# Attention's output normalised instead of its probabilities, with the reciprocals taken through DRAM

## The chip, the cores and the metric

The kernel runs on one core of a Trainium2 chip. The core has five engines with queues of their own that work in order: TensorE (PE: matmuls and transposes, into PSUM), VectorE (DVE), ScalarE (ACT), GpSimd (POOL) and SyncE (SP), which here only issues DMAs. The metric is device time in microseconds. The kernel before takes 586.34 us, the median of three runs (584.38 to 586.84).

## The reference

Causal attention over 2 batches x 12 heads, 448 tokens, head size 64; its output, as 896 rows of 768, goes through two dense blocks.

```
scores = q @ k.T / 8;  masked above the diagonal
attn   = exp(scores - max);  attn = attn / (sum(attn) + 1e-9)
x      = attn @ v                        # 896 x 768
h      = ((x @ w1) * (x @ w2)) @ w3 @ w_out
h      = h @ w_in;  out = (h * clip(h + 3, 0, 6) / 6) @ w_out2
```

## The kernel before

**Stages.** Attention comes first and ends at about 153 us of the span. Beside it the program multiplies w3 and w_out into one matrix (tile `pw`, written to DRAM as `product_of`), which depends on no activation; these 384 matmuls fill TensorE where attention leaves it free, and go on after it. Then come the products of x with w1 and w2 in a scheme of seven products per block (`pa`, tiles paX, paY, paZ), the product with the combined matrix (`px`), and the two matrices of the last block (`pg`, `po`). The dense stages hold every operand as a high and a low part and run three matmuls per product.

**Attention.** Two heads make a unit; there are twelve units u, six of each batch. A unit has seven tiles t of 64 queries. Its 128 partitions are 64 queries of two heads. `scores` (L392) runs for t = 6 down to 0: a matmul of q's tile with the keys up to it into a PSUM bank `s` (L399); VectorE adds the mask, writes the scores `z` to SBUF and leaves the row's extreme in `sums` (L402); ScalarE takes the exponential into the buffer `prb` and leaves the row's sum in `sums` (L406). `normalise` (L411) is called three times per unit, for tiles 6 and 5, for 4 and 3, and for 2 to 0: VectorE adds 1e-9 and takes the reciprocals (L417, L418), and GpSimd multiplies each tile of `prb` by its column of reciprocals (L425). `p_t` (L435) transposes the 16 blocks of 128x128 on TensorE in four groups (L447) and copies them to `pt` (L455 on ScalarE, L459 on VectorE). `p_v` (L463) multiplies `pt` with v into one PSUM bank `o` (L472), which holds 64 rows of either head and the 448 queries as columns, and turns it into `xt`: a high part on ScalarE (L489) and a low part on VectorE (L490), or plain copies (L487, L494) for the second batch, where the differences of L564 are formed from x itself.

**Weights.** Each weight tile comes as 64-bit numbers (`w3r`, `wrr`, `w1r`, `w2r`) and is converted by ScalarE (L266), VectorE (L269, L271, L273) and split into parts (L250 on ScalarE, L253 on VectorE or GpSimd).

**The order of the work.** Operations are declared with an engine, a cost, what they read and write, and a rank. A planner (`Plan.issue`) plays them through with these costs and hands each engine, whenever it is free, the ready operation of lowest rank. The result is a fixed order for every engine; on the chip each engine follows it and waits where an operand is not there. SP's queue is fixed in the same way: a DMA whose condition isn't met holds up all that stand behind it.

Of the kernel before, what the change touches and what calls it, by code (L numbers as in the profile page):

```python
# [23 lines left out]

GROUPS = (5, 3)
# [127 lines left out]
def attention_moe_moe2(ctx: ExitStack, tc, q, k, v, w1, w2, w3, w_out, v_in, v_out, out):  # L153
# [43 lines left out]
    three, small = consts[:, :1], consts[:, 1:4]  # L197
# [144 lines left out]
    qr, kr, vr, qs, ks, sums, pt, pr = {}, {}, {}, {}, {}, {}, {}, {}  # L342
# [68 lines left out]
    def normalise(u, t0, t1):  # L411
        sm, pb = sums[u], pr[u]
        rank = u + (TQ - t0) * 0.05
        acc = [sm.at((1, t)) for t in range(t0, t1)]

        def go():
            nc.vector.tensor_tensor(sm[:, 2, t0:t1], sm[:, 1, t0:t1], small[:, :t1 - t0], ALU.add)  # L417
            nc.vector.reciprocal(sm[:, 1, t0:t1], sm[:, 2, t0:t1])  # L418

        plan.op("dve", 0.47, go, writes=acc, rank=rank)  # L420

        def scale(t):
            n = (t + 1) * T
            s = pb[:, OFF[t]:OFF[t] + n]
            nc.gpsimd.tensor_tensor(s, s, sm[:, 1, t:t + 1].to_broadcast([P, n]), ALU.mult)  # L425

        for t in reversed(range(t0, t1)):
            plan.op("pool", pool((t + 1) * T), lambda t=t: scale(t),
                    reads=[sm.at((1, t))], writes=[pb.at(t)], rank=rank)
# [32 lines left out]
    def p_v(u):  # L462
# [23 lines left out]
        if b and p < HK:  # L486
            plan.op("act", act(S), lambda: nc.scalar.copy(f32(t[:, 0]), ps[:, :S]), reads=[ps], writes=[t.at(0)], rank=rank)  # L487
        else:
            plan.op("act", act(S), lambda: nc.scalar.copy(t[:, HI], ps[:, :S]), reads=[ps], writes=[t.at(0)], rank=rank)  # L489
            plan.op("dve", dve(S), lambda: nc.vector.tensor_tensor(t[:, LO], ps[:, :S], f32(t[:, HI]), ALU.subtract),  # L490
                    reads=[ps, t.at(0)], writes=[t.at(1)], rank=rank)
        if b and p >= HK:
            bf[p] = plan.tile(lambda: wrp.tile([P, S], F32, tag=f"bf{p}", name=f"bf{p}"), f"bf{p}", 1)
            plan.op("act", act(S), lambda: nc.scalar.copy(bf[p][:, :], ps[:, :S]), reads=[ps], writes=[bf[p]], rank=rank)  # L494
# [3 lines left out]
    for u in range(n_u):  # L498
        load(u)
        top = TQ  # L500
        for t in reversed(range(TQ)):
            scores(u, t)
            if t in (*GROUPS, 0):
                normalise(u, t, top)
                top = t
# [357 lines left out]
```

## Time and profile before

| | us |
|---|---|
| median of three runs | 586.34 (584.38 to 586.84) |
| profiled execution: its own time | 585.28 |
| its span in the trace | 583.5 |
| TensorE busy | 559.1 (96%) |
| VectorE busy | 408.9 (70%) |
| ScalarE busy | 282.4 (48%) |
| GpSimd busy | 147.1 (25%) |

The profiled execution is 1.06 us under the median and 1.8 us over its span. Busy time counts an engine's instructions, including time in which an instruction stands on an engine and waits; TensorE's ends are modelled. A group of instructions is given as line, engine, operation, names and shapes, count, busy time and mean of one, and after the second bar the idle time of the engine ahead of it with what ended it.

### The profile page before, as it was taken

The numbers are of one execution on the slowest core, as the hardware profiler recorded it, in microseconds if no ns is written. First come the engines' busy times: TensorE is split into PE (matmuls) and PEld (weight loads), VectorE is DVE, ScalarE is ACT, GpSimd is POOL, SyncE is SP. The second block draws the span as 40 slices with busy tenths as digits, with TensorE's granted clock in tenths as the row PEclk, the third lists the DMA queues.
The fourth block names the chain that finished last, engine by engine and source line by source line (L and its number), as shares of the span: only waits on it lengthen the run. The fifth ranks groups of instructions, "written<-read, shape, count | busy, mean of one in ns | idle before, by whom it ended". The sixth has DMA issues, their size and how long they took to land.

```text
span 583.5 us, 7873 instructions
## 1 busy us (share of the span) xinstructions
PE 559.1 (96%) x2900; PEld 496.1 (85%) x2900; DVE 408.9 (70%) x691; ACT 282.4 (48%) x532; POOL 147.1 (25%) x143
## 2 busy tenths in 40 slices
PE   7797989899999999999999999999999999999997
PEld 5575666677899998888999999999999999999996
DVE  4989898898795989999845447877878865452000
ACT  5777778777652454554523325555556623130100
POOL 3878787698121223321210000000000000000000
PEclk9889989999999999999999999999999999999999
DMA  8565566543432223432233114333344442440000
GB/s 314 186 207 185 183 243 207 172 169 124 120 123 64 99 109 108 148 115 82 77 123 109 51 58 162 110 108 109 110 144 145 144 158 91 136 144 16 17 31 33
DMA packets 22855, 73.39 MB, mean 126 GB/s; under 512 B 2080, under 2 KB 11296, under 8 KB 20256
## 3 DMA queue, kind: packets, MB, share of 16 engines
q1 hardware_dynamic: 22816, 72.88, 36.4%
q8 instruction: 23, 0.38, 0.3%
q14 instruction: 16, 0.13, 0.1%
HBM read 66.98 MB, written 5.90 MB: 125 GB/s over the span
## 4 chain that ended last, share of the span: by engine, by line
PE 73%; DVE 14%; POOL 3%; DMA 3%; issue 3%; ACT 2%; SPq 0%; DVEq 0%; POOLq 0%; ACTq 0%
PE po L793 20%; PE pg L617 20%; PE px L752 10%; PE pw L535 8%; PE paX L678 4%; PE s L399 4%; POOL prb L425 3%; PE ptp L447 3%; PE o L472 2%; PE paZ L678 2%; DVE z L402 2%; DVE wd L253 2%; DMA ks<-in_k 1%; PE paY L678 1%; DMA w1r<-in_moe_w 1%
## 5 line engine op out<-in xcount | busy, mean ns | idle before, releaser
L793 PE MATMUL po<-g,vo 128*128 128x448 f32 x576 | 115.4, 362 | 0.0
L617 PE MATMUL pg<-x2t,vi 128*128 128x448 f32 x576 | 115.4, 362 | 0.0
L617 PEld LDWEIGHTS pg<-x2t,vi 128*128 128x128 f32 x576 | 108.0, 187 | 7.2
L793 PEld LDWEIGHTS po<-g,vo 128*128 128x128 f32 x576 | 108.0, 187 | 7.2
L425 POOL TENSOR_TENSOR prb<-prb,sums 128x448 f32<-128x448 f32 (+6 forms) x84 | 75.3, 922 | 29.1 <-DVE sums L418 24.9
L535 PE MATMUL pw<-wr,w 128*128 128x384 f32 x384 | 76.6, 349 | 0.0
L535 PEld LDWEIGHTS pw<-wr,w 128*128 128x128 f32 x384 | 66.5, 190 | 1.7 <-issue 0.5
L399 PE MATMUL s<-ks,qs 128*128 128x448 f32 (+6 forms) x168 | 52.5, 425 | 9.7 <-DVE sums L402 7.2
L752 PE MATMUL px<-ab,wp 128*128 128x448 f32 x288 | 57.8, 362 | 0.0
L752 PEld LDWEIGHTS px<-ab,wp 128*128 128x128 f32 x288 | 54.0, 187 | 3.6
L406 ACT ACTIVATE prb<-z,sums 128x448 f32<-128x448 f32 (+6 forms) x84 | 42.2, 506 | 7.2 <-DVE sums L402 7.1
L399 PEld LDWEIGHTS s<-ks,qs 128*128 128x128 f32 x168 | 29.5, 202 | 19.0 <-DVE sums L402 10.0
L402 DVE CUSTOM_DVE_ANT_0 z<-s,maskb 128x448 f32<-128x448 f32 (+6 forms) x84 | 33.1, 418 | 13.6 <-PE s L399 8.6
L638 ACT ACTIVATE r<-pg,consts 128x448 f32<-128x448 f32 x32 | 20.4, 636 | 33.3 <-PE pg L617 33.3
L447 PEld LDWEIGHTS ptp<-ident,prb 128*128 128x128 f32 x192 | 23.0, 146 | 13.9 <-POOL prb L425 9.1
L447 PE MATMUL ptp<-ident,prb 128*128 128x128 f32 x192 | 27.8, 287 | 5.9 <-POOL prb L425 5.8
L455 ACT COPY pt<-ptp 128x512 f32<-128x512 f32 (+1 forms) x48 | 25.1, 562 | 16.4 <-PE ptp L447 16.0
L266 ACT ACTIVATE vor<-vor 128x1024 f32<-128x1024 f32 x12 | 13.9, 1155 | 39.4 <-DMA vor<-in_moe_w_out 39.4
L312 POOL TENSOR_TENSOR w2r<-w2r 128x384 f32<-128x384 f32 x8 | 9.9, 1244 | 74.3 <-DVE w2r L273 51.2
L640 DVE SCALAR_TENSOR_TENSOR g<-r,pg 128x448 f32<-128x448 f32 x32 | 19.8, 619 | 12.5 <-ACT r L638 12.4
L653 DVE COPY out<-po 128x448 f32<-128x448 f32 x6 | 3.7, 624 | 35.3 <-PE po L793 35.1
L472 PE MATMUL o<-pt,vr 128*64 128x448 f32 (+3 forms) x192 | 26.4, 394 | 0.2
(110 smaller groups left out, 890.5 us busy)
## 6 DMA issues: line engine op xcount, KB each, us to landing
vir<-in_moe_w_in SPq DMA_DIRECT2D x16, 768.0 KB, 4.2
vor<-in_moe_w_out SPq DMA_DIRECT2D x12, 1024.0 KB, 5.0
w3r<-in_moe_w SPq DMA_DIRECT2D x8, 1024.0 KB, 5.2
wrr<-in_moe_w_out SPq DMA_DIRECT2D x8, 768.0 KB, 4.5
w1r<-in_moe_w SPq DMA_DIRECT2D x8, 768.0 KB, 5.7
w2r<-in_moe_w SPq DMA_DIRECT2D x8, 768.0 KB, 4.4
qs<-in_q SPq DMA_DIRECT2D x12, 448.0 KB, 3.9
vr<-in_v SPq DMA_DIRECT2D x12, 256.0 KB, 2.7
```

The costliest lines, as they stand in the source:

```text
L399: plan.op("pe", pe4(n), lambda: nc.tensor.matmul(ps[:, :n], qs[u][:, t].rearrange("p h i -> p (h i)"), ks[u][:, :n], start=True, stop=True ...
L402: plan.op("dve", dve(n) + 0.09, lambda: nc.vector.tensor_tensor_reduce(out=z[:, :n], in0=ps[:, :n], in1=maskb[:, S - n:], scale=-SCALE, sc ...
L406: plan.op("act", act(n, True) + 0.2, lambda: nc.scalar.activation(pb[:, OFF[t]:OFF[t] + n], z[:, :n], AF.Exp, bias=sm[:, 0, t:t + 1], scal ...
L425: nc.gpsimd.tensor_tensor(s, s, sm[:, 1, t:t + 1].to_broadcast([P, n]), ALU.mult)
L447: nc.tensor.transpose(ps[:w, i * P:(i + 1) * P], pb[:, OFF[t] + kb * P:OFF[t] + kb * P + w], ident)
L455: plan.op("act", act(cut), lambda: nc.scalar.copy(dst()[:, :cut], ps[:, :cut]), reads=[ps], writes=[d.at((g, 0))], rank=rank)
L472: nc.tensor.matmul(ps[T * j:T * j + T, kb * P:S], vr[u][:w, kb, j, :], d[:w, base[kb]:base[kb] + TQ - 2 * kb, j, :], start=kb == 0, stop=k ...
L535: nc.tensor.matmul(ps[:, :W], weight(n, a, kk), hls[1 + kk][:, c, h * W:(h + 1) * W], start=kk == 0 and a == c, stop=kk == KF - 1 and a == LO)
L617: nc.tensor.matmul(ps[:, :S], weight(n, a, kk), x(kk, c), start=st, stop=sp)
L678: nc.tensor.matmul(ps[:, :S], hl[:, a, off + kk * P:off + (kk + 1) * P], t[:, c], start=first and kk == 0 and a == c, stop=kk == HK - 1 an ...
L752: nc.tensor.matmul(ps[m, b][:, :S], weight(n, a, kk), ab[kk][:, c, cols(b)], start=kk == 0 and a == c, stop=kk == KF - 1 and a == LO)
L793: nc.tensor.matmul(ps[:, :S], weight(n, a, kk), gt[k][:, c, cols(b)], start=k == 0 and a == c, stop=k == KF2 - 1 and a == LO)
```

## The change

The call of `normalise` goes, and with it GpSimd's multiplication of the probabilities: the transposes take the exponentials as they are. Once per unit, behind its seven tiles, `invert` adds 1e-9 to the seven sums and takes their reciprocals on VectorE. They lie with queries along the partitions and are wanted along the columns of `o`; so one DMA writes the 128x7 reciprocals to a piece of DRAM (`line`, 28 bytes from each partition), and two DMAs read it back, one per head, each spreading a row of 448 numbers over 64 partitions (`inv`, in the scratch tag "a2"). In `p_v` VectorE multiplies the bank `o` by `inv`, reading `inv` at a step of seven numbers, and writes x. Where high and low parts are wanted, ScalarE casts x and GpSimd subtracts; for the second batch's first three units x itself is all that is needed.

```diff
--- before.py
+++ after.py
@@ -21,8 +21,6 @@
 
 BANKS = {'s': 3, 'pt': 2, 'o': 1}
 DENSE_BANKS = 2
-
-GROUPS = (5, 3)
 
 AHEAD = 0.5
 
@@ -194,7 +192,7 @@
     dp = ctx.enter_context(tc.tile_pool(name="dp", bufs=1, space=bass.MemoryType.DRAM))
     pd = ctx.enter_context(tc.tile_pool(name="pd", bufs=DENSE_BANKS, space=PSUM))
     consts = cp.tile([P, 8], F32, name="consts")
-    three, small = consts[:, :1], consts[:, 1:4]
+    three, small = consts[:, :1], consts[:, 1:]
 
     ctx.enter_context(tc.manual_schedule())
 
@@ -339,7 +337,7 @@
 
     seq = [(b, p) for b in range(B) for p in range(NP)]
     n_u = len(seq)
-    qr, kr, vr, qs, ks, sums, pt, pr = {}, {}, {}, {}, {}, {}, {}, {}
+    vr, qs, ks, sums, pt, pr, inv = {}, {}, {}, {}, {}, {}, {}
 
     def scratch(tag, name):
         return plan.tile(lambda: xp.tile([P, S], F32, tag=tag, name=name, bufs=2), tag, 2)
@@ -408,25 +406,26 @@
             bias=sm[:, 0, t:t + 1], scale=-1.0, accum_out=sm[:, 1, t:t + 1]),
             reads=[z, sm.at((0, t))], writes=[pb.at(t), sm.at((1, t))], rank=rank + RANK["exp"])
 
-    def normalise(u, t0, t1):
-        sm, pb = sums[u], pr[u]
-        rank = u + (TQ - t0) * 0.05
-        acc = [sm.at((1, t)) for t in range(t0, t1)]
+    def invert(u):
+
+        sm = sums[u]
+        rank = u + (TQ - 1) * 0.05
 
         def go():
-            nc.vector.tensor_tensor(sm[:, 2, t0:t1], sm[:, 1, t0:t1], small[:, :t1 - t0], ALU.add)
-            nc.vector.reciprocal(sm[:, 1, t0:t1], sm[:, 2, t0:t1])
-
-        plan.op("dve", 0.47, go, writes=acc, rank=rank)
-
-        def scale(t):
-            n = (t + 1) * T
-            s = pb[:, OFF[t]:OFF[t] + n]
-            nc.gpsimd.tensor_tensor(s, s, sm[:, 1, t:t + 1].to_broadcast([P, n]), ALU.mult)
-
-        for t in reversed(range(t0, t1)):
-            plan.op("pool", pool((t + 1) * T), lambda t=t: scale(t),
-                    reads=[sm.at((1, t))], writes=[pb.at(t)], rank=rank)
+            nc.vector.tensor_tensor(sm[:, 2], sm[:, 1], small, ALU.add)
+            nc.vector.reciprocal(sm[:, 1], sm[:, 2])
+
+        plan.op("dve", 0.47, go, writes=[sm], rank=rank)
+        line = dp.tile([2, T * TQ], F32, name=f"line{u}")
+        lh = Handle(plan, None, None, 0)
+        lh.ap = line
+        plan.op("sp", 0.6, lambda: nc.sync.dma_start(
+            line.rearrange("j (i t) -> (j i) t", t=TQ), sm[:, 1]), reads=[sm], writes=[lh], rank=rank)
+        inv[u] = scratch("a2", f"inv{u}")
+        for j in range(2):
+            plan.op("sp", 0.6, lambda j=j: nc.sync.dma_start(
+                inv[u][T * j:T * j + T], line[j:j + 1].to_broadcast([T, S])),
+                reads=[lh], writes=[inv[u].at(j)], rank=rank)
 
 
     order = [(kb, t) for kb in range(4) for t in range(2 * kb, TQ)]
@@ -484,25 +483,29 @@
                     writes=[ps], rank=rank)
         t = plan.tile(lambda: xp.tile([P, 2, S], F32R, tag=f"x{p}_{b}", name=f"xt{p}_{b}"), f"x{p}_{b}", 1)
         if b and p < HK:
-            plan.op("act", act(S), lambda: nc.scalar.copy(f32(t[:, 0]), ps[:, :S]), reads=[ps], writes=[t.at(0)], rank=rank)
+            x, write = lambda: f32(t[:, 0]), t.at(0)
+        elif b:
+            bf[p] = plan.tile(lambda: wrp.tile([P, S], F32, tag=f"bf{p}", name=f"bf{p}"), f"bf{p}", 1)
+            x, write = lambda: bf[p][:, :], bf[p]
         else:
-            plan.op("act", act(S), lambda: nc.scalar.copy(t[:, HI], ps[:, :S]), reads=[ps], writes=[t.at(0)], rank=rank)
-            plan.op("dve", dve(S), lambda: nc.vector.tensor_tensor(t[:, LO], ps[:, :S], f32(t[:, HI]), ALU.subtract),
-                    reads=[ps, t.at(0)], writes=[t.at(1)], rank=rank)
-        if b and p >= HK:
-            bf[p] = plan.tile(lambda: wrp.tile([P, S], F32, tag=f"bf{p}", name=f"bf{p}"), f"bf{p}", 1)
-            plan.op("act", act(S), lambda: nc.scalar.copy(bf[p][:, :], ps[:, :S]), reads=[ps], writes=[bf[p]], rank=rank)
+            xf = scratch("a1", f"xf{u}")
+            x, write = lambda: xf[:, :], xf
+        plan.op("dve", dve(S), lambda: nc.vector.tensor_tensor(
+            x().rearrange("p (t i) -> p t i", i=T), ps[:, :S].rearrange("p (t i) -> p t i", i=T),
+            inv[u][:, :].rearrange("p (i t) -> p t i", t=TQ), ALU.mult),
+                reads=[ps, inv[u]], writes=[write], rank=rank)
+        if not b or p >= HK:
+            plan.op("act", act(S, True), lambda: nc.scalar.copy(t[:, HI], x()), reads=[write], writes=[t.at(0)], rank=rank)
+            plan.op("pool", pool(S), lambda: nc.gpsimd.tensor_tensor(t[:, LO], x(), f32(t[:, HI]), ALU.subtract),
+                    reads=[write, t.at(0)], writes=[t.at(1)], rank=rank)
         xt[p, b] = t
 
     setup()
     for u in range(n_u):
         load(u)
-        top = TQ
         for t in reversed(range(TQ)):
             scores(u, t)
-            if t in (*GROUPS, 0):
-                normalise(u, t, top)
-                top = t
+        invert(u)
         for g in range(4):
             p_t(u, g)
         p_v(u)
```

How the orders differ, at three places. `o` and `s` are PSUM banks, `z` the masked scores, `sums` a unit's extremes and sums, `wrr` tiles of weights, `pt` the transposed probabilities. Line numbers after the change are two lower up to L408 and one lower in `p_t` and `p_v` up to L474.

VectorE, around the reciprocals in the middle of attention, before (the additions of one unit stand in three places; the low part of x is taken from `o`):

```order
L402 ISA z_0_526,sums_412<-s_0_471,maskb 128x64
L402 ISA sums_412 128x1
L417 TENSOR_TENSOR sums_412<-sums_412,consts 128x2
L418 RECIPROCAL sums_412<-sums_412 128x2
L402 ISA z_6_540,sums_541<-s_6_477,maskb 128x448
L402 ISA sums_541 128x1
L402 ISA z_5_549,sums_541<-s_5_499,maskb 128x384
L402 ISA sums_541 128x1
L490 TENSOR_TENSOR xt_0_546<-o_506,xt_0_546 128x448
L402 ISA z_4_559,sums_541<-s_4_530,maskb 128x320
```

and after, at the same place:

```order
L400 ISA z_4_552,sums_531<-s_4_527,maskb 128x320
L400 ISA sums_531 128x1
L415 TENSOR_TENSOR sums_419<-sums_419,consts 128x7
L416 RECIPROCAL sums_419<-sums_419 128x7
L493 TENSOR_TENSOR xf_567<-o_482,inv_488 128x448
L267 TENSOR_SCALAR wrr_512<-wrr_512 128x768
L269 SCALAR_TENSOR_TENSOR wrr_416<-wrr_416 128x768
L458 COPY pt_547<-ptp_3_570 64x128
L271 SCALAR_TENSOR_TENSOR wrr_416<-wrr_416 128x768
L400 ISA z_3_605,sums_531<-s_3_549,maskb 128x256
L400 ISA sums_531 128x1
```

The multiplication of one unit's output (`xf` from `o_482` and `inv_488`) stands right behind the reciprocals of the next unit (`sums_419`); behind it come conversions of weights, the copy of pt and the next maximum (z_3).

SP, the queue of one unit in the middle of attention, before:

```order
L244 DMA wrr_444<-in_moe_w_out 128x1536
L359 DMA qs_479<-in_q 128x896
L360 DMA ks_488<-in_k 128x448
L361 DMA vr_524<-in_v 128x512
L244 DMA wrr_537<-in_moe_w_out 128x1536
L244 DMA wrr_579<-in_moe_w_out 128x1536
```

and after:

```order
L422 DMA line_133<-sums_310 128x7
L357 DMA qs_472<-in_q 128x896
L358 DMA ks_479<-in_k 128x448
L426 DMA inv_488<-line_133 64x448
L359 DMA vr_500<-in_v 128x512
L426 DMA inv_488<-line_133 64x448
L242 DMA wrr_512<-in_moe_w_out 128x1536
```

The row to DRAM (`line_133`) stands ahead of the loads of q, k and v of the unit three later (`qs_472`, `ks_479`, `vr_500`), the first spread between k and v, the second behind v.

TensorE, the last output matmuls of attention, before:

```order
L447 MATMUL ptp_3_1603<-ident,prb_88 128x128 x3
L447 MATMUL ptp_3_1603<-ident,prb_88 64x128
L472 MATMUL o_1610<-pt_1584,vr_1243 64x448 x2
L472 MATMUL o_1610<-pt_1584,vr_1243 64x320 x2
L535 MATMUL pw_1_1551<-wr_850,w_1200 128x384 x3
L535 MATMUL pw_1_1551<-wr_861,w_1200 128x384 x3
L535 MATMUL pw_0_1625<-wr_329,w_1309 128x384 x3
L472 MATMUL o_1610<-pt_1584,vr_1243 64x192 x2
L472 MATMUL o_1610<-pt_1584,vr_1243 64x64 x2
```

and after:

```order
L446 MATMUL ptp_2_1473<-ident,prb_88 128x128 x4
L446 MATMUL ptp_3_1482<-ident,prb_88 128x128 x3
L446 MATMUL ptp_3_1482<-ident,prb_88 64x128
L538 MATMUL pw_0_1468<-wr_377,w_1149 128x384 x3
L538 MATMUL pw_0_1468<-wr_490,w_1149 128x384 x3
L471 MATMUL o_1501<-pt_1465,vr_1180 64x448 x2
L471 MATMUL o_1501<-pt_1465,vr_1180 64x320 x2
L471 MATMUL o_1501<-pt_1465,vr_1180 64x192 x2
L471 MATMUL o_1501<-pt_1465,vr_1180 64x64 x2
L538 MATMUL pw_0_1468<-wr_533,w_1149 128x384 x3
```

In the whole order 65 triples of product matmuls (`pw`) stand ahead of attention's last matmul before the change, and 51 after it.

## Rows read from the trace of the kernel before

**Rows 1.** The page, part 1: busy us (share), instructions.

```profile
PE 559.1 (96%) x2900; PEld 496.1 (85%) x2900; DVE 408.9 (70%) x691; ACT 282.4 (48%) x532; POOL 147.1 (25%) x143
```

**Rows 2.** Table by stage: length, busy us, granted clock, DMA share, GB/s.

```profile
5.40:45.00 39.60, 33.92 (x166) 22.58 (x164) 32.97 (x94) 28.55 (x73) 27.57 (x27) 0.87 0.66 238
45.00:100.00 55.00, 48.37 (x278) 34.31 (x276) 49.20 (x137) 42.74 (x114) 43.94 (x44) 0.97 0.61 213
100.00:153.00 53.00, 49.51 (x310) 38.58 (x308) 45.29 (x95) 37.65 (x85) 37.12 (x30) 1.00 0.40 132
153.00:186.00 33.00, 33.00 (x194) 33.00 (x191) 27.37 (x37) 15.00 (x28) 8.42 (x5) 1.00 0.39 120
```

**Rows 3.** The chain that ended last, attention's end: start, us, what.

```profile
152.33 0.74 PE o L472 x8
153.07 32.96 PE pw L535 x189
```

**Rows 4.** TensorE's waits to 150 us: us, times, longest; last line, after.

```profile
PE s L399 <- DVE sums L402: 7.2, 7, 2.2
PE ptp L447 <- POOL prb L425: 5.8, 8, 1.5
...
PE paX L678 <- DVE wa L253: 3.7, 4, 1.4
```

**Rows 5.** Groups on GpSimd to 153 us; last line, from 153 to 300.

```profile
L425 POOL TENSOR_TENSOR prb<-prb,sums 128x448 f32<-128x448 f32 (+6 forms) x84 | 75.3, 922 | 29.1 <-DVE sums L418 24.9 <-DVE sums L417 3.0 <-ACT w3r L266 0.4
L253 POOL TENSOR_TENSOR w<-w3r,w 128x1024 fp32r<-128x1024 f32 x7 | 18.3, 2615 | 2.9 <-ACT w L250 2.9
L253 POOL TENSOR_TENSOR wr<-wrr,wr 128x768 fp32r<-128x768 f32 x8 | 15.5, 1941 | 1.7 <-ACT wr L250 1.7
...
L698 POOL TENSOR_TENSOR u<-u,c 128x448 f32<-128x448 f32 x8 | 11.2, 1399 | 31.3 <-DVE u L696 23.5 <-ACT ab L704 7.8
```

**Rows 6.** VectorE to 153 us, groups; last two, durations ns min/median/max.

```profile
L402 DVE CUSTOM_DVE_ANT_0 z<-s,maskb 128x448 f32<-128x448 f32 (+6 forms) x84 | 33.1, 418 | 13.6 <-PE s L399 8.6 <-ACT prb L406 3.2 <-POOL prb L425 1.2
L417 DVE TENSOR_TENSOR sums<-sums,consts 128x2 f32<-128x2 f32 (+1 forms) x36 | 14.5, 403 | 0.0
L273 DVE SCALAR_TENSOR_TENSOR wrr<-wrr 128x768 uint32<-128x768 uint32 x8 | 11.1, 1390 | 0.0
...
L418 DVE RECIPROCAL sums<-sums 128x2 f32<-128x2 f32 (+1 forms) x36 | 6.1, 170 | 1.2
L490 DVE TENSOR_TENSOR xt<-o,xt 128x448 fp32r<-128x448 f32 x8 | 4.9, 618 | 2.3 <-ACT xt L489 2.3
L459 DVE COPY pt<-ptp 64x128 f32<-64x128 f32 x12 | 3.3, 277 | 2.6 <-ACT pt L455 2.6
...
L273 DVE SCALAR_TENSOR_TENSOR w1r<-w1r 128x768 uint32<-128x768 uint32 x2 | 1.9, 953 | 0.0
...
L417 DVE TENSOR_TENSOR sums<-sums,consts x36: 144/256/1539, 10.5 to 141.7; 128x2 f32<-128x2 f32 x24, 128x3 f32<-128x3 f32 x12
L269 DVE TENSOR_SCALAR w3r<-w3r x8: 678/1047/2148, 9.4 to 131.4; 128x1024 uint32<-128x1024 uint32 x8
```

**Rows 7.** Casts on ScalarE: from PSUM to 153 us; from SBUF, ns min/median/max.

```profile
L489 ACT CAST xt<-o 128x448 fp32r<-128x448 f32 x8 | 4.2, 527 | 6.7 <-PE o L472 6.7
...
L704 ACT CAST ab<-p x8: 565/570/571, 202.8 to 292.3; 128x448 fp32r<-128x448 f32 x8
```

**Rows 8.** SP's wait; k's issue (ns); landings of k, v, product.

```profile
SPq L361 <- PE o L472: 40.4, 9, 6.2
...
L360 SPq DMA_DIRECT2D ks<-in_k x12: 416/424/647, 1.2 to 109.7; - x12
...
DMA to landing us min/median/max: 3.2/4.2/8.1
...
DMA to landing us min/median/max: 2.5/2.7/8.3
...
DMA to landing us min/median/max: 2.0/3.2/5.6
```

## The prediction

> **What bounds the kernel now.** I read the page first: TensorE is busy for 96% of the span [rows 1]. A share of 96% says that no more than 583.5 - 559.1 = 24.4 us of the span is idle time of TensorE, so the next question was where it lies. The table by stage answers [rows 2]: of the 39.6 us from 5.4 to 45 TensorE lacks 5.7, from 45 to 100 it lacks 6.6, from 100 to 153 it lacks 3.5; from 153 to 186 nothing; 3.7 us follow in the next stage, where VectorE's split of wa is late [rows 4]. So 15.8 us lie in the attention stage, which the change is about, and which ends at 153.07 us, where the chain turns into one run of 189 matmuls of the weights' product [rows 3]. [...]
>
> Who made TensorE wait came third [rows 4]: 7.2 us for VectorE's running maxima (the banks of the scores), 5.8 us for GpSimd's scaling of the probabilities (8 waits of the transposes). GpSimd's rows say why it is late: 84 multiplications of 922 ns are 75.3 of its work in the stage [rows 5]. VectorE is the busiest engine of the stage beside TensorE: 33.0 + 49.2 + 45.3 = 127.5 of 147.6 us [rows 2].
>
> **The change part by part.** *TensorE's own work* is the same in kind and number. In the order 195 of the 384 product matmuls stood ahead of attention's last matmul, and 153 do now; the other 42 go behind it, at 32.96/189 = 0.174 us each [rows 3] 7.3 us. That is no gain and no loss: the attention stage ends 7.3 us earlier for it and the run behind it is 7.3 us longer. What counts is idle time and clock.
>
> *GpSimd loses* the 84 multiplications, 75.3 us, and gains nine subtractions of 128x448 (the low parts of x), at 1.4 us of the nearest row, the product of u and c [rows 5], 12.6 us. With the weights' 18.3 + 15.5 its work in the stage falls from about 109 to about 46 us. The 5.8 us that the transposes waited for it [rows 4] go; late next are the exponentials themselves on ScalarE, which stood before GpSimd in the same chain, so that the wait can only shorten. I take -5.8; the bounds are 0 (ScalarE takes its place whole) and -5.8.
>
> *VectorE loses* 24 of 36 pairs of addition and reciprocal. An addition took 403 ns in the mean, though it handles two or three numbers in a lane; its shortest took 144 ns [rows 6], so the rest is standing still until ScalarE's sum is there. 14.5 + 6.1 = 20.6 us become 12 x (0.4 + 0.18) = 7.0: 13.6 us less. Beside GpSimd its other work is slow too: the shift of a w3 tile took 678 ns at the least, 1047 in the median and 2148 at most, with GpSimd's work changing beside it and nothing else in it [rows 6]. Eight such shifts at the median are 8 x 0.37 = 3.0 us over their shortest, and the last joins of wrr 8 x (1.390 - 0.953 of the w1r tiles of the same size) = 3.5 [rows 6]. Of shifts and joins there are six such groups of eight in the stage, so that I take 17 us of excess in all (estimate from these two, with the differences left out); with GpSimd's work at 46/109, 58% of it goes, 10 us. It gains twelve multiplications of the output in place of nine subtractions of 618 ns [rows 6]: 3 x 0.62 = 1.9 us. So VectorE goes from 127.5 to about 106 us of work. Its share of a stage of some 130 us is then 80%, below TensorE's, and I let half of the 7.2 us of waits for the maxima go: -3.6, bounds 0 and -7.2.
>
> The new multiplication reads the reciprocals at a step of 28 bytes; no row shows such a step. Its nearest row is the subtraction from the same bank, 618 ns, and I take that; twice as long would be the upper end, 12 x 0.62 = 7.4 us more on an engine that has some 25 us free, nothing or at most 6.8 us on the path (11 of them in the loop below). [...] Were the multiplication doubled, the sum below would be up to 6.8 us higher; by the row it stays.
>
> *ScalarE* loses the six plain copies of the output (0.53 us each, as its casts [rows 7]) and casts nine times from SBUF instead of from PSUM, 0.57 for 0.53 [rows 7]: -2.8 us, beside other work, nothing on the path.
>
> *The clock.* Lost now: 0.13 x 33.9 + 0.03 x 48.4 = 5.9 us [rows 2]. With fewer idle gaps a part comes back. The loads of the first units stay as late as they are, so I take a third, -2.0; bounds 0 and -5.9.
>
> *The DMAs* are what is added: per unit one of 128 rows of 28 bytes to DRAM and two that spread 1,792 bytes over 64 partitions, 36 in all, at 0.42 us of SP each (k's load [rows 8]), 15 us of SP beside other work. Bytes: 12 x 2 x 64 x 1,792 = 2.75 MB in a stage that moves 132 to 238 GB/s [rows 2], hidden. What can cost is the chain and the queues. On SP the row waits for the reciprocals and the first spread for the row, and loads of q, k and v for the unit three later stand behind and between them. The second spread stands behind that load of v, which waits for the end of this unit's output matmuls: SP already stood 40.4 us behind v in this way [rows 8]. On VectorE the multiplication stands right behind the reciprocal of the next unit, and behind it the conversions, the next maxima and the copy of pt, for which the next output matmul waits. So there is a loop from one unit's output to the next one's: issues of v and of the spread 2 x 0.42, landing 2.7 (v's median [rows 8]), multiplication 0.62, two conversion steps 2.4 (1.39 each beside GpSimd, 0.95 without [rows 6]; I take 1.2), a maximum 0.42, the copy of pt 0.28 [rows 6], the second half of the output matmuls 0.74 [rows 3]: 8.0 us. A unit takes (153.1 - 5.4)/12 = 12.3 us now; on my sum it will take 11.0. So the loop is hidden with 3.0 us to spare, and shows where the spread lands later than 5.7 us. Landings of like DMAs: 2.0 to 5.6 us for the product's stores, 2.5 to 8.3 for v [rows 8]. At 2.0 the cost is nothing; at 8.3 in all eleven turns it is 11 x 2.6 = 29 us. Both rows' medians are near 3, so I take the low end with one or two late landings, +3.0.
>
> *The sum.* 585.28 us is the profiled execution's own time (span 583.5 and 1.8 around it); -5.8 - 3.6 - 2.0 + 3.0 = -8.4 gives 576.9. The median of the three runs is 586.34, 1.06 higher, inside their 584.38 to 586.84; on its scale the forecast is 578.0. Behind 153 us I expect nothing but the shift: the 3.7 us of waits for wa [rows 4] are untouched by the change, and VectorE has 5.6 us free from 153 to 186 [rows 2], with 7.3 us more of the product's run to get ready in.
>
> **The rivals** (all times on the scale of the median).
> 1. The gaps close altogether: -5.8 - 7.2 - 5.9 = -18.9 and no new wait, 567.4. For it: GpSimd loses over half its work, and VectorE with it. Against: in-order engines rarely lose all waits, and the load of k at the start stays.
> 2. The round trip decides: slower. Place: VectorE's multiplication, with the maxima and the copy of pt behind it. If the spreads land after 7.2 us in the mean, 11 x 1.5 = 16.5 us stand in place of the 3.0: 591.5. It wipes out the gain from a mean landing of 5.7 + 11.4/11 = 6.7 us. For it: the maxima of 8.1 and 8.3 us of k and v [rows 8], and that loads of q, k and v stand ahead of the second spread. Against: the medians of 2.7 to 4.2 there. [...]
> 3. The wait only moves: ScalarE's exponentials take GpSimd's place, VectorE gives nothing, and the clock stays: 583.5 to 586. For it: ScalarE is busy 109 of 147.6 us [rows 2], and GpSimd waits for its sums. Against: GpSimd's 75 us follow on the exponentials today and nothing takes their place in the chain.
>
> **How the numbers follow.** Forecast 0.54 (its own range 573 to 583), rival 1 0.14, rival 2 0.18, rival 3 0.14. The 80% range runs from 568, all but the full gain, to 592, all but the upper part of rival 2. A measurement here tells half a per cent, 2.9 us, from no change: faster (below 583.4) is the forecast and rival 1, 0.68; same is rival 3, 0.14; slower is rival 2, 0.18.
>
> **What would show it.** Right: no wait of transposes for GpSimd; the addition's mean near its shortest in most instances; the shift of a w3 tile near 0.7 us; the attention's last matmul near 137 us; a granted clock above 0.87 in the first 40 us; the run of product matmuls near 40 us. Wrong: idle time of VectorE before the multiplication, ended by a DMA, of more than some 10 us in total, or a multiplication of 1.2 us; scores or output matmuls that wait for the maxima or the copy of pt behind it; loads of q and k that come late because SP stands behind the row to DRAM; or waits for wa that grow beyond 3.7 us.

## The result: slower by 0.4 to 0.7%

Twenty runs of the changed kernel have a median of 588.22 us (583.84 to 590.16), twenty of the kernel before 585.09 (583.20 to 586.84). The ratio is 1.0052, with a 95% interval from 1.0036 to 1.0068: 3.0 us slower, where 8.4 us faster was forecast. The profiled execution of the changed kernel took 585.17 us, one of its fastest; so the two traces, with spans of 583.4 and 583.5 us, show a tie, and the last 3 us have to come from the comparisons of many runs.

The table by stage of the kernel after (its columns are those of [rows 2]: length, busy us of PE, PEld, DVE, ACT, POOL, granted clock, DMA share, GB/s):

```profile
5.40:45.00 39.60, 34.37 (x188) 22.83 (x187) 30.38 (x88) 30.43 (x81) 12.16 (x7) 0.96 0.79 272
45.00:100.00 55.00, 46.99 (x259) 32.81 (x259) 39.72 (x103) 40.04 (x103) 19.11 (x11) 0.91 0.67 210
100.00:153.00 53.00, 49.17 (x306) 40.12 (x307) 46.99 (x90) 35.06 (x84) 17.81 (x8) 1.00 0.53 173
153.00:186.00 33.00, 33.00 (x192) 33.00 (x191) 29.41 (x37) 15.04 (x27) 9.10 (x6) 1.00 0.35 104
```

Against [rows 2], GpSimd's work is down from 108.6 to 49.1 us, VectorE's from 127.5 to 117.1. Yet TensorE lacks 39.60 - 34.37, 55.00 - 46.99 and 53.00 - 49.17 us, 17.1 in all, in these three stretches, where it lacked 15.8. The DMA share is up in each (0.66 to 0.79, 0.61 to 0.67, 0.40 to 0.53). The granted clock rose from 0.87 to 0.96 in the first stretch and fell from 0.97 to 0.91 in the second, where the idle time is.

The chain that ended last, at attention's end (start, us, what), then TensorE's waits (us, times, longest), which answer to [rows 3, 4]:

```profile
143.92 2.03 PE o L471 x16
145.95 40.25 PE pw L538 x231
```

```profile
PE s L397 <- DVE sums L400: 14.6, 14, 2.9
PE paX L681 <- DVE wa L251: 3.7, 4, 1.4
...
PE o L471 <- DVE pt L458: 0.8, 1, 0.8
```

Attention ends 7.1 us earlier, about the 7.3 us of product matmuls that moved behind it; both traces start the next stage (paX) at 186.0 to 186.2 us. The 5.8 us in which the transposes waited for GpSimd are gone, and the waits for the maxima have grown by 7.4, from 7.2 to 14.6.

What makes VectorE late stands in its groups to 153 us (busy, mean ns, idle before and what ended it), and in its waits:

```profile
L493 DVE TENSOR_TENSOR xf<-o,inv 128x448 f32<-128x448 f32 x6 | 5.8, 960 | 5.3 <-DMA inv<-line 5.3
L567 DVE TENSOR_TENSOR xt<-xt,xt 128x448 f32<-128x448 f32 x6 | 11.9, 1984 | 0.1
L267 DVE TENSOR_SCALAR w3r<-w3r 128x1024 uint32<-128x1024 uint32 x8 | 6.1, 758 | 2.1 <-DMA w3r<-in_moe_w 2.1
L415 DVE TENSOR_TENSOR sums<-sums,consts 128x7 f32<-128x7 f32 x12 | 4.6, 385 | 0.0
```

```profile
DVE xf L493 <- DMA inv<-line: 5.3, 2, 3.4
DVE w3r L267 <- DMA w3r<-in_moe_w: 2.1, 3, 1.5
DVE xt L493 <- DMA inv<-line: 1.9, 1, 1.9
DVE wrr L267 <- DMA wrr<-in_moe_w_out: 1.7, 2, 1.4
```

VectorE waits 7.2 us in three places for the spread reciprocals and 3.8 us for weights; before, it waited 1.4 us for weights (L269). One instance of the first, from the timelines of SP, VectorE and TensorE (start, us, engine, line; the idle time before in brackets):

```profile
28.67 0.45 SPq L426 DMA_DIRECT2D inv<-line  x1
31.28 0.20 DVE L416 RECIPROCAL sums<-sums 128x7 f32<-128x7 f32 x1
34.92 0.95 DVE L493 TENSOR_TENSOR xf<-o,inv 128x448 f32<-128x448 f32 x1 [3.44 <-DMA inv<-line]
35.79 0.42 DVE L400 CUSTOM_DVE_ANT_0 z<-s,maskb 128x256 f32<-128x256 f32 x1
36.27 0.69 PE L397 MATMUL s<-ks,qs 128*128 128x64 f32 x2 [2.94 <-DVE sums L400]
```

The spread was issued at 28.67 behind the loads of q, k and v, and landed 6.2 us later. VectorE, in order, stood 3.44 us at the multiplication with a maximum behind it, and TensorE's scores stood 2.94 us for want of a bank. The second kind:

```profile
80.20 1.86 POOL L251 TENSOR_TENSOR wr<-wrr,wr 128x768 fp32r<-128x768 f32 x1 [3.06 <-ACT wr L248]
82.39 0.33 SPq L422 DMA_DIRECT2D line<-sums  x1
82.76 0.42 SPq L242 DMA_DIRECT2D w3r<-in_moe_w  x1
88.71 0.70 DVE L267 TENSOR_SCALAR w3r<-w3r 128x1024 uint32<-128x1024 uint32 x1 [1.54 <-DMA w3r<-in_moe_w]
89.87 1.45 PE L397 MATMUL s<-ks,qs 128*128 128x384 f32 x4 [1.62 <-DVE sums L400]
```

A load of weights goes out when GpSimd has finished with a buffer, here at 80.20 + 1.86 = 82.06. In front of it on SP stood the row to DRAM, which waited for reciprocals, so it went out at 82.76, up to 0.7 us late, and VectorE could start on its data 5.9 us later. VectorE stood 1.54 us for them and TensorE 1.62, at a place that has nothing to do with reciprocals; at most 0.7 of the 1.54 us come from SP's standing. SP's waits to 153 us show how often it stands behind a row or a spread:

```profile
SPq L422 <- DVE sums L416: 36.9, 12, 5.1
...
SPq L426 <- DMA line<-sums: 11.2, 7, 4.3
```

### The profile page after: what moved, and what is told of

It reads as the page before. It is cut to its first block, busy times and chain, and to the rows that moved or that the text cites. A ratio compares the mean times of both kernels' runs of the same rounds, so it can differ in the third digit from the quotient of the medians.

```text
span 583.4 us, 7791 instructions
## 1 busy us (share of the span) xinstructions
PE 557.7 (96%) x2900; PEld 496.6 (85%) x2900; DVE 400.3 (69%) x646; ACT 279.1 (48%) x526; POOL 88.2 (15%) x68
## 4 chain that ended last, share of the span: by engine, by line
PE 67%; DVE 10%; issue 2%; DMA 1%; ACT 0%; DVEq 0%; ACTq 0%; SPq 0%
PE po L796 20%; PE pg L620 20%; PE px L755 10%; PE pw L538 8%; PE paX L681 4%; PE paZ L681 2%; DVE wd L251 2%; PE paY L681 1%; DVE ab L709 1%; DVE w1r L269 1%; DVE w1r L310 1%; PE s L397 1%; DMA w2r<-in_moe_w 1%; PE o L471 1%; PE ptp L446 1%
## 5 line engine op out<-in xcount | busy, mean ns | idle before, releaser
L538 PE MATMUL pw<-wr,w 128*128 128x384 f32 x384 | 78.9, 354 | 0.1
L397 PE MATMUL s<-ks,qs 128*128 128x448 f32 (+6 forms) x168 | 50.4, 418 | 16.2 <-DVE sums L400 14.6
L404 ACT ACTIVATE prb<-z,sums 128x448 f32<-128x448 f32 (+6 forms) x84 | 42.1, 506 | 14.7 <-DVE sums L400 14.5
L251 POOL TENSOR_TENSOR w<-w3r,w 128x1024 fp32r<-128x1024 f32 x8 | 22.3, 2800 | 51.5 <-ACT w L248 51.5
L471 PEld LDWEIGHTS o<-pt,vr 128*64 128x64 f32 (+1 forms) x192 | 11.4, 138 | 16.7 <-issue 8.4
L645 ACT ACTIVATE g<-g 128x448 fp32r<-128x448 f32 x32 | 18.6, 580 | 13.9 <-DVE g L643 13.9
```

The lines of the kernel that those rows point to most:

```text
L251: plan.op(eng, pool(size) if eng == "pool" else dve(size), lambda: e.tensor_tensor(hl[:, LO, at_:at_ + size], x(), f32(hl[:, HI, at_:at_ + ...
L397: plan.op("pe", pe4(n), lambda: nc.tensor.matmul(ps[:, :n], qs[u][:, t].rearrange("p h i -> p (h i)"), ks[u][:, :n], start=True, stop=True ...
L404: plan.op("act", act(n, True) + 0.2, lambda: nc.scalar.activation(pb[:, OFF[t]:OFF[t] + n], z[:, :n], AF.Exp, bias=sm[:, 0, t:t + 1], scal ...
L471: nc.tensor.matmul(ps[T * j:T * j + T, kb * P:S], vr[u][:w, kb, j, :], d[:w, base[kb]:base[kb] + TQ - 2 * kb, j, :], start=kb == 0, stop=k ...
L538: nc.tensor.matmul(ps[:, :W], weight(n, a, kk), hls[1 + kk][:, c, h * W:(h + 1) * W], start=kk == 0 and a == c, stop=kk == KF - 1 and a == LO)
```

## The experiments

All times are medians; ratios are to the kernel before, run on the same chip in turn, with a 95% interval in brackets. With 585.1 us for a ratio of 1, 0.01 is 5.9 us. A trace shows one execution, which lay up to 3.9 us from the median here (a_fixed_dma).

### What GpSimd's multiplications cost, and what the regrouping alone does

**b_noscale** (before):

```diff
-            nc.gpsimd.tensor_tensor(s, s, sm[:, 1, t:t + 1].to_broadcast([P, n]), ALU.mult)
+            pass
```

> The kernel before with its 84 multiplications on GpSimd left out (the output is not normalised); every other instruction and its place is kept. It asks whether GpSimd's work was on the path at all. If it was, as the prediction had it, the 5.8 us of waits and part of VectorE's slowness go: 575 to 579. If the waits only move on to ScalarE and VectorE in an unchanged order: 583 to 586, against 585.1 before.

Measured 572.61, ratio 0.9775 (0.9746 to 0.9805): 13.2 us, more than expected. The gain that the change was after is there.

```profile
5.40:45.00 39.60, 35.30 (x192) 23.48 (x190) 34.53 (x112) 32.99 (x89) 11.11 (x5) 1.00 0.75 266
```

```profile
PE s L399 <- DVE sums L402: 5.7, 7, 1.8
```

No wait of the transposes is left, and the same run of 189 product matmuls starts at 138.35 instead of 153.07, 14.7 us earlier. Shorter waits make 8.5 of these: 5.8 for GpSimd, 1.5 for the maxima, 1.2 for a load of k. The clock makes about the rest: granted 1.00 in all three stretches, it gives back the 5.9 us that were lost to it before.

**b_pool1** (before, reciprocals once a unit):

```diff
-GROUPS = (5, 3)
+GROUPS = ()
```

> The kernel before with only the regrouping of the change: the reciprocals of a unit once and not in three groups, the multiplications on GpSimd as before. Theory: VectorE's 13.6 us less are worth little by themselves, since GpSimd's multiplications now begin 7 tiles late and the transposes wait for them: 585 to 592, waits of the transposes for GpSimd above the 5.8 us of before. Rival (VectorE's time is the bound): 578 to 583.

592.01, ratio 1.0124 (1.0100 to 1.0147), and

```profile
PE ptp L447 <- POOL prb L425: 12.2, 7, 3.5
```

So the regrouping cost time here, where the probabilities wait for it: the transposes' waits doubled, from 5.8 to 12.2 us, and whatever VectorE's shorter work gave was less than that. The two were not separated.

### What the round trip costs: taken away in steps

**a_fixed_nodma** (after): no row, no spread; the multiplication reads `fixed`, a tile filled once at the start.

```diff
-            inv[u][:, :].rearrange("p (i t) -> p t i", t=TQ), ALU.mult),
+            fixed[:, :].rearrange("p (i t) -> p t i", t=TQ), ALU.mult),
...
-        plan.op("sp", 0.6, lambda: nc.sync.dma_start(
-            line.rearrange("j (i t) -> (j i) t", t=TQ), sm[:, 1]), reads=[sm], writes=[lh], rank=rank)
+        plan.op("sp", 0.6, lambda: None, reads=[sm], writes=[lh], rank=rank)
...
-            plan.op("sp", 0.6, lambda j=j: nc.sync.dma_start(
-                inv[u][T * j:T * j + T], line[j:j + 1].to_broadcast([T, S])),
+            plan.op("sp", 0.6, lambda: None,
```

> The changed kernel with its 36 DMAs of reciprocals left out; the multiplication reads a tile that is filled once (other values, same order of all that is left). If the round trip through DRAM ate the gain (VectorE stands 7.2 us for inv, SP 36.9 us for the reciprocals with weight loads behind it), about 8 us go: 578 to 581, against 588.2 for the changed kernel. If VectorE's slower multiplication and GpSimd's subtractions ate it: 586 to 588.

576.76, ratio 0.9864 (0.9832 to 0.9896): 8.0 us faster than before, somewhat more than expected.

```profile
45.00:100.00 55.00, 50.26 (x287) 35.26 (x285) 46.46 (x117) 43.15 (x112) 19.41 (x10) 0.94 0.64 217
```

```profile
PE s L399 <- DVE sums L402: 8.0, 10, 1.9
```

```profile
136.29 40.25 PE pw L538 x231
```

Attention ends 9.7 us earlier than in the changed kernel, with the same order of instructions; the waits for the maxima are 8.0 instead of 14.6, and VectorE waits 0.7 us for weights instead of 3.8. The granted clock is 1.00 in the first stretch and 0.94 in the second, so 0.06 x 50.3 = 3.0 us are lost to it.

**a_fixed_dma** (after): only the first of these edits, the one on the multiplication; the DMAs stay with their waits.

> The changed kernel with all its DMAs, but the multiplication reads a tile that is filled once, so that VectorE never waits for a DMA of reciprocals. It splits the round trip: if VectorE's waits for inv are what costs, 583 to 585 and close to the run without DMAs; if SP's standing in front of the loads is what costs, 587 to 588 as the changed kernel.

584.68, ratio 1.0001 (0.9977 to 1.0025). VectorE no longer waits for the reciprocals, and this gives 3 us. SP still does, and VectorE waits for weights. The trace is of an execution of 588.59 us, 3.9 over the median, so the sizes of its waits are not those of the step:

```profile
DVE w3r L267 <- DMA w3r<-in_moe_w: 8.0, 6, 1.9
```

```profile
SPq L424 <- DVE sums L418: 43.6, 12, 7.4
```

**a_traffic** (after): the same DMAs at the same places, none waiting for reciprocals; the multiplication reads `fixed` here too. The rows are filled from `fixed`, and the spreads read a row of DRAM, `row0`, that is written once at the start.

```diff
+        nc.sync.dma_start(row0.rearrange("j (i t) -> (j i) t", t=TQ), fixed[:, :TQ])
-            line.rearrange("j (i t) -> (j i) t", t=TQ), sm[:, 1]), reads=[sm], writes=[lh], rank=rank)
+            line.rearrange("j (i t) -> (j i) t", t=TQ), fixed[:, :TQ]), reads=[sm], writes=[lh], rank=rank)
...
-                inv[u][T * j:T * j + T], line[j:j + 1].to_broadcast([T, S])),
+                inv[u][T * j:T * j + T], row0[j:j + 1].to_broadcast([T, S])),
```

> The changed kernel with as many DMAs of the same sizes in the same places of SP's queue, but none waits for reciprocals: the 28-byte rows come from a tile that is filled once, the spreads from a DRAM row written once, and the multiplication reads the filled tile. If SP's standing behind the reciprocals (36.9 us) and behind the row (11.2 us) is what holds the loads back, it comes close to the run without DMAs (576.8): 576 to 579. If the transfers themselves crowd the loads out (weights landing in 6.3 us instead of 5.2), it stays at 583 to 585, as the run with all DMAs and no wait of VectorE (584.7).

583.75, ratio 0.9985 (0.9957 to 1.0012), in the second range. Its first added line spoiled it: that DMA stood at the head of SP's queue behind a fill on GpSimd, so that the first load left at 4.57 us and the first scores ran at 9.51 us instead of about 5.5. The next run takes that DMA off SP.

**a_traffic2**:

```diff
-        nc.sync.dma_start(row0.rearrange("j (i t) -> (j i) t", t=TQ), fixed[:, :TQ])
+        nc.gpsimd.dma_start(row0.rearrange("j (i t) -> (j i) t", t=TQ), fixed[:, :TQ])
```

> The changed kernel with its 36 DMAs at the same places of SyncE's queue and of the same sizes, but none waits for reciprocals, and the multiplication reads a tile filled once (output not normalised). As a_traffic, but the DRAM row is filled by a DMA of GpSimd's queue, so that the first loads leave SyncE at once and not at 4.6 us. Theory (what is paid back has three parts: VectorE's waits for the reciprocals 3.5 us, SyncE's queue standing behind the line DMA about 5 us, the transfers themselves about 3 us): about 580, between 578.5 and 581.5. Rival (only the transfers' crowding counts, SyncE's standing costs nothing): 583 to 585, as a_traffic was, its late start being made up for later.

581.67, ratio 0.9946 (0.9931 to 0.9962): 0.2 us above the theory's range, and below the rival's. The transfers, with no wait in front of them and nobody waiting for what they bring, cost 0.0082, 4.8 us. In this is also the time of their issue on SP, 24 of 0.45 and 12 of 0.43 us, some 16 us; no run separates the two. Part of it shows in the trace: weights land later (median of a w3 load 6.2 us, against 5.5 in a_fixed_nodma), and VectorE waits 6.4 us for them, against 0.7:

```profile
DVE w3r L267 <- DMA w3r<-in_moe_w: 3.9, 3, 1.5
DVE wrr L267 <- DMA wrr<-in_moe_w_out: 2.5, 4, 1.3
```

```profile
PE o L475 <- DVE pt L462: 2.8, 2, 2.3
```

The output matmuls wait 2.8 us for the copy of pt, which stands behind such a conversion on VectorE (0.4 in a_fixed_nodma); the granted clock is 0.96 and 0.94 in the first two stretches, against 1.00 and 0.94.

**a_contig** (after): the same tile read in storage order (the reciprocals meet the wrong columns).

```diff
-            inv[u][:, :].rearrange("p (i t) -> p t i", t=TQ), ALU.mult),
+            inv[u][:, :].rearrange("p (t i) -> p t i", t=TQ), ALU.mult),
```

> The changed kernel with the multiplication reading inv in storage order instead of at a step of 28 bytes (the reciprocals meet the wrong columns). If the step is what makes it 0.96 us instead of 0.62, it falls to about 0.62 and 12 x 0.35 = 4.2 us of VectorE go; on the path 0 to 4: 584 to 588. [...]

586.31, ratio 1.0024 (0.9999 to 1.0049), 1.6 us less than the change in the ratios, with intervals that overlap. That the step sets the multiplication's duration, and not GpSimd beside it, is plain, at 593 ns against 960:

```profile
L493 DVE TENSOR_TENSOR xf<-o,inv 128x448 f32<-128x448 f32 x6 | 3.6, 593 | 1.5 <-DMA inv<-line 1.5
```

### Complete versions that avoid a part of the price

**a_late** (after): the planner is told that the row is ready 3 us later and the spreads 1.5 us later, so that other loads stand ahead of them on SP.

```diff
-ready[j] = max(ready[j], free[e] + (0.0 if near else self.LATENCY.get(e, 0.12)))
+ready[j] = max(ready[j], free[e] + (0.0 if near else self.LATENCY.get(e, 0.12)) + self.late.get(j, 0.0))
...
+        plan.late[i] = 3.0
...
+            plan.late[i] = 1.5
```

> The changed kernel complete, but the planner is told that the row goes out 3 us later and each spread 1.5 us later than it thought, so that it puts loads of q, k, v and weights ahead of them on SP and the multiplication later on VectorE (63 instead of 51 triples of product matmuls ahead of attention's end). If waiting in the queues is the cause, 578 to 584; if the DMAs' presence is the cause, 586 to 589.

586.89, ratio 1.0026 (1.0007 to 1.0046), in the second range. SP's wait for reciprocals fell from 36.9 to 3.0 us. VectorE's waits for weights did not go, though:

```profile
DVE w3r L268 <- DMA w3r<-in_moe_w: 6.1, 3, 3.4
...
DVE xf L496 <- DMA inv<-line: 4.4, 5, 2.0
```

**a_poolq** (after): the 36 DMAs issued by GpSimd, planned as a queue of its own.

```diff
-    LATENCY = {"pe": 0.2, "sp": 2.2}
+    LATENCY = {"pe": 0.2, "sp": 2.2, "q": 3.0}
...
-        plan.op("sp", 0.6, lambda: nc.sync.dma_start(
+        plan.op("q", 0.6, lambda: nc.gpsimd.dma_start(
```

> The changed kernel complete, its 36 DMAs issued by GpSimd instead of SP, so that no load stands behind them. If SP's queue is the cause: 577 to 581, less what GpSimd's own waits in front of the weights' low parts cost. If the round trip as seen by VectorE or the traffic is the cause: 584 to 588.

595.48, ratio 1.0176 (1.0141 to 1.0212), slower than either range. The DMAs now stand in the queue of an engine with longer work in it (its split of a w3 tile takes 2.7 us), and the round trip decides: the output matmuls wait for the multiplication of the unit before.

```profile
DVE xf L493 <- DMA inv<-line: 8.3, 3, 3.8
```

```profile
PE o L471 <- DVE xf L493: 9.2, 4, 4.3
```

**a_pe2, a_pe1** (after): no DRAM; TensorE spreads the reciprocals. a_pe1 leaves out the lower part (h = 1).

```diff
+                rep[:, h], fold[:, :].unsqueeze(1).to_broadcast([P, TQ, T]),
+                f32(rh[:, h]).unsqueeze(2).to_broadcast([P, TQ, T]), ALU.mult),
...
+                rs[:, :S], pair[:, :], rep[:, h].rearrange("p t i -> p (t i)"), start=h == 0, stop=h == 1),
...
+        plan.op("act", act(S), lambda: nc.scalar.copy(bc[:, :], rs[:, :S]), reads=[rs], writes=[bc], rank=u + RANK["pt"] + 0.2)
...
-            inv[u][:, :].rearrange("p (i t) -> p t i", t=TQ), ALU.mult),
+            bc[:, :].rearrange("p (t i) -> p t i", i=T), ALU.mult),
```

> The changed kernel without the trip through DRAM: GpSimd multiplies a repeated identity by the reciprocals' upper and lower parts (24 of 448 columns), TensorE spreads them over the partitions by two matmuls of 448 columns a unit, ScalarE copies the bank to SBUF, and the multiplication reads it in storage order. Complete. Theory (the round trip through DRAM is what eats the gain of 12 us): the kernel without the DMAs took 576.8; 24 matmuls of about 0.2 us add 4.8, reading in order takes about 2 off: about 580, between 577 and 583, faster than the kernel before. Rival (any work put back on GpSimd, here 24 by 1.5 us, or on ScalarE, 12 by 0.53 us, costs as much as the trip did): 585 to 589.

> As a_pe2 with the upper part of the reciprocals alone, so they are rounded to the short form in which TensorE reads them: 12 multiplications on GpSimd and 12 matmuls instead of 24. Theory: 2.4 us less of TensorE and 18 us less of GpSimd than a_pe2: about 577.5, between 575 and 581. Rival: as a_pe2's, 584 to 588. If a_pe1 and a_pe2 differ by more than 3 us, GpSimd's work beside VectorE is what is paid, and not TensorE's.

587.82, ratio 1.0055 (1.0035 to 1.0074), and 586.12, ratio 1.0027 (1.0010 to 1.0043). The theory fell and the rival's range held: taking the trip away did not bring the gain here, where other engines had to do the spreading. In a_pe1:

```profile
L434 POOL TENSOR_TENSOR rep<-fold,rh 128x448 fp32r<-128x448 f32 x12 | 19.5, 1623 | 34.4 <-DVE rh L430 18.4 <-DMA wrr<-in_moe_w_out 11.9 <-PE s L405 3.5
...
PE s L405 <- DVE sums L408: 9.7, 7, 3.4
```

The two differ by 1.7 us, less than the 3 that was to accuse GpSimd. Which of the added pieces (12 copies of 540 ns on ScalarE, the matmuls, the plan that they changed) costs most was not separated.

**b_dve3, b_dve1** (before): the multiplications on VectorE; b_dve1 with GROUPS = () besides.

```diff
-            nc.gpsimd.tensor_tensor(s, s, sm[:, 1, t:t + 1].to_broadcast([P, n]), ALU.mult)
+            nc.vector.tensor_scalar(s, s, sm[:, 1, t:t + 1], None, ALU.mult)
```

> The kernel before, complete, with its 84 multiplications of the probabilities on VectorE (a scalar per partition, in place) instead of GpSimd, planned at the cost of VectorE's shift L269. Estimate from that shift's shortest rows (678 ns for 1024 columns): 0.06 us and 0.62 ns a column, 20 us of VectorE in all, against 75 us of GpSimd. Theory (broadcasting the reciprocals over partitions is what ate the change's gain; GpSimd's work is worth 12 us to whoever removes it without that): 572.6 of b_noscale and 5 to 10 for the 20 us of VectorE: about 579, between 575 and 584, faster than before. Rival (the multiplications cost the same wherever they stand, VectorE becomes the bound): 586 or more.

> As b_dve3, with the reciprocals of a unit taken once and not in three groups (as in the changed kernel): 24 fewer additions and 24 fewer reciprocals on VectorE (before: 36 of 403 and 36 of 170 ns; after: 12 of 385 and 12 of 201, so 13.6 us less), but the probabilities of a unit are all ready later. Theory: VectorE carries only some 6 us more than in b_noscale: about 575, between 572 and 581. Rival (the unit's latency counts, the transposes wait for the multiplications): 584 or more, with waits of the transposes for VectorE above 5 us.

594.06, ratio 1.0144 (1.0114 to 1.0174), and 585.81, ratio 1.0012 (0.9993 to 1.0030). My estimate of the multiplication was too low (436 to 451 ns in the mean, not 240):

```profile
L425 DVE TENSOR_SCALAR prb<-prb,sums 128x448 f32<-128x448 f32 (+6 forms) x84 | 34.2, 451 | 0.4
```

Both missed the theory's range. With 34 us on VectorE instead of 75 on GpSimd, and no broadcast at all, b_dve1 ties with before.

**b_mix, b_mix2** (before): two groups; the late, short multiplications on VectorE, the others on GpSimd. In b_mix2 both 4s of the diff are 3s.

```diff
-GROUPS = (5, 3)
+GROUPS = (4,)
...
+            if t < 4:
+                nc.vector.tensor_scalar(s, s, sm[:, 1, t:t + 1], None, ALU.mult)
```

> The kernel before, complete, with reciprocals in two groups (query tiles 6 to 4, then 3 to 0); the multiplications of the first group (384 columns in the mean) stay on GpSimd, those of the second (160 in the mean) go to VectorE. Worked out from b_dve1's and before's rows: VectorE gets 48 multiplications of about 0.33 us, 16 us, and loses 12 additions and 12 reciprocals, 7 us; GpSimd loses 48 of about 0.55 us, 27 of its 75 us. Theory (the transposes' wait for GpSimd, 5.8 us, can be had without the broadcast): 580, between 576 and 584. Rival (VectorE's time is the bound and contention stays): 585 to 592.

> As b_mix with the second group of three tiles (2 to 0, 128 columns in the mean) on VectorE: 36 multiplications of about 0.29 us, 10.5 us, less 7 us of additions and reciprocals, so VectorE carries only some 3 us more than before; GpSimd loses 36 of about 0.45 us, 16 us. Theory: as b_mix, 578 to 584. Rival: 585 to 592.

588.11, ratio 1.0051 (1.0033 to 1.0069), and 592.24, ratio 1.0115 (1.0091 to 1.0139): the rival both times. The transposes waited for VectorE instead of GpSimd, 3.6 us in b_mix, and in b_mix2

```profile
PE ptp L450 <- DVE prb L426: 9.0, 7, 2.9
```

None of these complete versions beats the kernel before.

## Why the prediction was wrong

**The step that failed is the round trip's price, +3.0 in the sum.** The ladder of experiments measures it, from the ratios. A step is known to about 2 us (1.7 to 2.1, from the intervals of its two ratios, which do not overlap):

| kernel | ratio | step, us | what comes in |
|---|---|---|---|
| before | 1 | | |
| a_fixed_nodma | 0.9864 | -8.0 | the change on the engines |
| a_traffic2 | 0.9946 | +4.8 | the transfers and their issue on SP |
| a_fixed_dma | 1.0001 | +3.2 | SP standing behind reciprocals and rows |
| after | 1.0052 | +3.0 | VectorE standing for the spreads |

The round trip costs 11.0 us. Without it my sum was -11.4; the engines' part measured -8.0. So -8.4 was forecast, -8.0 + 11.0 = +3.0 came out. Rival 2, slower, had the right sign, but not the price of 16.5 us: its trigger, a mean landing beyond 7.2 us, was not met. The spreads landed in 2.7 to 6.2 us:

```profile
DMA to landing us min/median/max: 2.7/3.6/6.2
```

The rows of 28 bytes landed in 1.4 to 6.2 us, median 3.5; the least lies under the 2.0 us of the shortest landing in [rows 8]. The step failed in two ways, and held in a third.

*"Bytes: ... hidden."* I compared GB/s and did not ask who waits for a load. The stage's loads of weights have three buffers, and SP issues one when a buffer comes free; where a load lands after VectorE's turn for it, VectorE stands (6.4 us in a_traffic2), and all behind it in its queue. The transfers cost 4.8 us without anyone waiting for their content.

*SP's standing.* I had seen that the row waits for the reciprocals, but followed only the loads of q, k, v and the second spread behind it. Behind the row stand the weights too: up to 0.7 us late in the instance at 82.76 above. I had named "loads of q and k that come late" as a sign; the loads that made VectorE wait were the weights'. That a_late took SP's wait away and gained no more than 1.5 us, against the 3.2 of this row, leaves open how much of it a better order could get back: its plan was another one in other places too.

*The multiplication's wait.* The loop from unit to unit was not what decided; I had set aside one or two late landings, 3.0 us, and three waits of 7.2 us in all came, of which about 3.0 reached the end. That single size was right, within the 2 us. It was one of three, and I took it for the whole.

**Half of the waits for maxima go, -3.6: wrong.** They doubled to 14.6 us: in the instances above the maximum stands in VectorE's queue behind what waits for a spread or a weight. Even without the DMAs (a_fixed_nodma) they were 8.0. This term is why the engines' part was -8.0 and not -11.4: in the trace of a_fixed_nodma the transposes' waits are gone (-5.8), the clock's loss is 3.0 us instead of 5.9 (-2.9, where -2.0 was forecast), and the waits for the maxima are 0.8 longer. These three make -7.9; that trace as a whole came 9.5 us under the one of before.

**VectorE to 106 us: 117.1.** The excess beside GpSimd fell where I looked: the shift of a w3 tile is at 758 ns (forecast near 0.7). The joins stayed, 1251 ns for wrr against 1390 in [rows 6], and the differences L567, which I had left out, went from 7.2 us (L564 before, six of 1195 ns) to 11.9. The timeline shows two of them beside the GpSimd work that is left:

```profile
122.29 5.91 POOL L251 TENSOR_TENSOR w<-w3r,w 128x1024 fp32r<-128x1024 f32 x2 [10.30 <-ACT w L248]
123.55 5.12 DVE L567 TENSOR_TENSOR xt<-xt,xt 128x448 f32<-128x448 f32 x2
128.87 0.81 PE L397 MATMUL s<-ks,qs 128*128 128x320 f32 x2 [1.92 <-DVE sums L400]
```

So contention did not scale with GpSimd's total time, as I had let it (46/109): that time fell from 108.6 to 49.1 us, and yet the differences rose from 1195 to 1984 ns each, with what stood beside them: the two above took 5.12 us. The addition's mean, too, stayed at 385 ns; the sign "near its shortest" failed, without weight in the sum.

**The step of 28 bytes, 0.62 us: wrong, within its upper end.** It took 0.96 to 1.01 us against 0.59 to 0.62 in storage order (a_contig), so 0.4 us each: 1.6 times, and not the doubling, which I had as the bound without a row for it. Why the step costs this, no run shows. Its effect on the end is 1.6 us by the ratios, not told from nothing.

**Right:** no wait of the transposes for GpSimd, -5.8; the 42 product matmuls move without gain or loss (40.25 us behind, 7.1 earlier); the waits for wa stay at 3.7 us; GpSimd at 49.1 us (about 46). The sign of the last matmul near 137 us failed: it came at 145.95.

**The clock:** above 0.87 in the first stretch, as said, but the second fell to 0.91, and 0.04 x 34.4 + 0.09 x 47.0 = 5.6 us are lost to it as against 5.9: the -2.0 did not come. That fewer gaps would bring a third of it back was my estimate, which no run shows; the three stretches had 0.96, 0.91 and 1.00. The two traces hide more than that. Both show a mean granted clock of 0.987 over the whole span. The twenty runs of the changed kernel have 0.985 in the mean (0.980 to 0.991), but the runs of the kernel before that stand beside the experiments 0.990 to 0.992, so that the trace of before was low for its kernel. 0.006 of 585 us is 3.5 us, an estimate from these means, and as much as the whole difference. Along the ladder the mean falls too: 0.993, 0.990, 0.987, 0.985. So a part of each of its three steps seems to reach the end as lower clock; by the same estimate 0.001 is 0.6 us. That TensorE's new idle time lowers it is not shown by itself; and the clock is not all, since a_late, at 0.992, is no faster than before.

## What to carry to other kernels

The 36 small DMAs added here cost 11.0 us: 4.8 as transfers and their issue, 3.2 with SP standing in its queue, 3.0 with VectorE standing in its own. So list every load behind the one that waits, and who waits for those, weights above all (VectorE stood 6.4 us for them in a_traffic2, against 0.7 without the DMAs). GpSimd's work was worth 13.2 us with nothing in its place (b_noscale) and 8.0 with the replacement on the engines alone (a_fixed_nodma); none of it was left once the replacement stood in the in-order queues that set the end. Leaving the work out, and the replacement's waits and transfers one at a time, measures both sides before a complete version is built. Contention between two engines is read instance by instance (what ran beside what), and did not shrink here in proportion to busy time (GpSimd's down to 49.1 of 108.6 us, the differences L567 up to 1984 ns from 1195).

## What was not expected of the hardware

A multiplication of probabilities by a scalar per partition on VectorE took 451 ns in the mean for 64 to 448 columns (b_dve1), but 549 for 64 to 192 columns in b_mix2, whose GpSimd still did the long ones:

```profile
L426 DVE TENSOR_SCALAR prb<-prb,sums 128x192 f32<-128x192 f32 (+2 forms) x36 | 18.2, 549 | 0.4
```

So it is not the columns that raise the mean. The timelines show what does: a unit's three multiplications took 0.68 us together where GpSimd did nothing beside them (three times, one of them at 124.90), and 2.58 us here:

```profile
111.49 2.58 DVE L426 TENSOR_SCALAR prb<-prb,sums 128x192 f32<-128x192 f32 x3
108.79 4.80 POOL L253 TENSOR_TENSOR w<-w3r,w 128x1024 fp32r<-128x1024 f32 x2
```

The median of b_mix2's 36 is 300 ns; the few beside a long GpSimd instruction make the mean.

The runs of the changed kernel also spread further (583.8 to 590.2 us) than those of before (583.2 to 586.8). The granted clock goes with it: 0.991 in the fastest of the twenty, 0.980 to 0.985 in the nine above 588.5. Which of the two causes the other, no run shows.
